# Second GEMM of the last two chunks as Strassen products of 128x256, behind the last first-GEMM sums

## The chip, the cores and the metric

The program runs on one core of a Trainium2 chip. The metric is device time in microseconds of one execution; the kernel before has a median of 893.36 us over three runs (893.23 to 894.0).

## The reference

Windowed attention (8 batches, 8 heads, 576 positions, 64 channels; half of the heads see 32 neighbours, half every fourth of 128) gives 4608 tokens of 512 channels, and these go through a feed-forward block:

```python
x = attn_out.transpose(0, 2, 1, 3).reshape(4608, 512)
h = x @ w_in                                          # w_in 512 x 2048
sp = np.maximum(h, 0.0) + np.log1p(np.exp(-np.abs(h)))
g = h * erf(sp)
out = g @ w_out                                       # w_out 2048 x 512
```

## The kernel before, in words

The tokens are cut into 9 chunks of 512 (`NCH`, `TOK`), the 2048 middle channels into 16 tiles of 128, taken in 8 pairs (`SPC = 8`). Every fp32 operand is held as a high and a low part in float32r, and a product of two operands is three matmuls: high x high, high x low, low x high. Each matmul carries its own load of 128x128 weights.

Chunks 0 to 2 are done plainly, together with most of the attention. Chunks 3 to 8 are done two at a time (`DOUBLES = 3`). For such a pair of chunks and one pair of channel tiles ("a double", `d` = 0 to 23, eight of them for each pair of chunks) the first GEMM `h = x @ w_in` is a Strassen-Winograd product: 7 products instead of 8, each 6 matmuls of 128x512, so 42 matmuls. `mm1_big(d, k)` issues product `k` into one of two PSUM banks, `h` and `bank` (called tx), in turn; `take_big(d, k)` adds it into the results on VectorE. `argument_big` is the softplus on ScalarE, then comes an Erf (both load a table first, since each needs another one), and `multiply_big` makes `g` in place. Of each double the tensor "A" belongs to the first chunk of the two and "B" to the second; B is stored to DRAM (`kept_g`) and read back later (`load_g`).

The second GEMM is plain: an item ("A", d) or ("B", d) is split into `ghi` and `glo` (`split_item`: ScalarE casts B, VectorE subtracts) and takes 24 matmuls of 128x512 into the four banks `acc`, which hold one chunk's 512 tokens by 512 outputs over the 8 items of a chunk.

The order is written out by hand in `period(i, late)`. Period `i` issues item `ITEMS[i]`'s 24 matmuls in four quarters of 6, and where `BIG` names a double for it also that double's 42 matmuls between the quarters. The doubles of the last pair of chunks (d = 16 to 23) are in periods 32 to 39, beside the items ("B", 14), ("B", 15) of the chunk pair before them and the first A items of their own; periods 40 to 49 hold only the ten items that are left. `AFT` names jobs that are put into periods: loads and sums of the right-hand operands of the next eight doubles. All large transfers are issued on SP's queue in program order; `load_left` brings a double's left operands (1.8 MB) two doubles ahead.

The program's functions that the change touches, with what calls them:

Of the kernel before, what the change touches and what calls it, by code (L numbers as in the profile page):

```python
# [139 lines left out]
def attn_moe_kernel(ctx: ExitStack, tc: tile.TileContext, qk, v, masks, eye, w_in, w_out, out):  # L140
# [630 lines left out]
    def take_big(d, k):  # L771
        y = (h, bank)[(7 * d + k) % 2]
# [30 lines left out]
    def multiply_big(kind_, d):  # L803
        e = hs[kind_, d]
        nc.vector.tensor_tensor(out=e, in0=e, in1=ls[kind_, d], op=ALU.mult)
# [319 lines left out]
```

## Time and profile before

| what | value |
|---|---|
| median of three runs | 893.36 us |
| the profiled execution | 892.89 us, of it a span of 890.9 us |
| granted TensorE clock, mean | 0.996 |
| TensorE matmul busy | 871.2 us, 98% |
| weight loads, beside it | 700.1 us, 79% |
| VectorE, ScalarE | 633.6 us (71%), 564.5 us (63%) |

The profile's times are those of one execution and count from its first instruction; the span ends with the last transfer. A matmul's recorded duration (390 ns for 128x512) is longer than its place in the stream, since matmuls are pipelined: what one costs is the distance between two starts. The profile calls the two banks of the first GEMM h and tx, those of the attention sp, and the four of the second GEMM acc.

### The profile page before, as it was taken

How to read it: one execution, taken by the hardware profiler on the slowest of the kernel's cores; microseconds unless marked ns; L12 is line 12 of the kernel's file. 1: busy time of each engine (PE TensorE's matmuls, PEld its weight loads, DVE VectorE, ACT ScalarE, POOL GpSimd, SP SyncE). 2: the span in 40 equal slices, each digit the busy share in tenths (PEclk: the TensorE clock that was granted, in tenths of full speed). 3: DMA queues.
4: the chain of work that ended last, by engine and by line, in shares of the span. 5: the costliest groups of instructions: out<-in, count | busy, mean ns of one | idle time of the engine just before them, and what ended most of it. 6: DMA issues, size and time to landing. Idle time of an engine off the chain costs nothing.

```text
span 890.9 us, 20870 instructions
## 1 busy us (share of the span) xinstructions
PE 871.2 (98%) x8134; PEld 700.1 (79%) x8134; DVE 633.6 (71%) x1575; ACT 564.5 (63%) x1271; POOL 81.3 (9%) x97
## 2 busy tenths in 40 slices
PE   7799999999999999999999999999999999999998
PEld 3367888888888888788887778888888888888886
DVE  5878888987798889777676765666566647576622
ACT  6889888897788886675677442774445434445321
POOL 2312201111111110011000000010000000000000
PEclk9999999999999999999999999999999999999999
DMA  8874446464658896566675741674449125442341
GB/s 272 295 245 154 128 155 197 148 232 127 222 203 270 295 341 248 172 224 221 204 239 200 272 176 54 209 237 161 166 155 361 51 83 200 166 154 83 140 144 48
DMA packets 66915, 170.41 MB, mean 191 GB/s; under 512 B 7680, under 2 KB 14592, under 8 KB 63744
## 3 DMA queue, kind: packets, MB, share of 16 engines
q1 hardware_dynamic: 66528, 168.55, 55.1%
q8 instruction: 64, 1.05, 0.5%
q10 hardware_dynamic: 288, 0.52, 0.2%
q14 instruction: 35, 0.29, 0.1%
HBM read 122.91 MB, written 46.14 MB: 190 GB/s over the span
## 4 chain that ended last, share of the span: by engine, by line
PE 91%; DVE 5%; DMA 1%; ACT 1%; issue 1%; POOL 1%; SPq 0%; DVEq 0%; POOLq 0%; ACTq 0%
PE acc L636 43%; PE h L768 13%; PE tx L768 13%; PE h L521 7%; PE tx L521 7%; PE sp L275 3%; PE sp L217 3%; PE sp L256 1%; PE h L357 1%; DMA qk<-in_qk_dram 1%; DMA v<-in_v_dram 1%; DVE w L458 0%; DVE w L459 0%; DVE prob L228 0%; DVE win L453 0%
## 5 line engine op out<-in xcount | busy, mean ns | idle before, releaser
L636 PE MATMUL acc<-wout_hi,ghi 128*128 128x512 f32 x576 | 227.4, 395 | 0.5 <-DVE ghi L611 0.4
L636 PE MATMUL acc<-wout_lo,ghi 128*128 128x512 f32 x576 | 224.6, 390 | 0.0
L636 PE MATMUL acc<-wout_hi,glo 128*128 128x512 f32 x576 | 159.0, 389 | 0.0
L636 PEld LDWEIGHTS acc<-wout_hi,ghi 128*128 128x128 f32 x576 | 108.2, 188 | 23.3 <-DVE ghi L611 0.9
L636 PEld LDWEIGHTS acc<-wout_hi,glo 128*128 128x128 f32 x576 | 108.1, 188 | 22.8
L636 PEld LDWEIGHTS acc<-wout_lo,ghi 128*128 128x128 f32 x576 | 108.2, 188 | 21.7
L251 POOL TENSOR_TENSOR prob<-prob,rinv 128x256 f32<-128x256 f32 x72 | 72.7, 1016 | 477.0 <-DVE ssum L249 239.9
L238 ACT ACTIVATE prob<-prob,nmax 128x64 f32<-128x64 f32 x288 | 96.3, 338 | 10.5 <-DVE nmax L228 10.3
L801 ACT ACT_TABLE_LOAD x24 | 30.8, 1283 | 93.0 <-DVE dbl L776 47.3
L768 PE MATMUL tx<-win 128*128 128x512 f32 x288 | 74.1, 392 | 0.8 <-DVE hc L778 0.8
L228 DVE CUSTOM_DVE_ANT_0 prob<-sp,cst 128x64 f32<-128x64 f32 x288 | 45.3, 220 | 40.6 <-ACT rows L317 28.2
L768 PE MATMUL h<-win 128*128 128x512 f32 x288 | 74.0, 392 | 0.0
L768 PEld LDWEIGHTS tx<-win 128*128 128x128 f32 x288 | 53.5, 188 | 12.7 <-DVE hc L778 1.2
L768 PEld LDWEIGHTS h<-win 128*128 128x128 f32 x288 | 53.4, 188 | 12.0 <-DVE dbl L778 0.8
L612 DVE TENSOR_TENSOR glo<-hc,ghi 128x512 fp32r<-128x512 f32 x50 | 34.5, 692 | 33.4 <-PE acc L636 22.6
L238 ACT ACTIVATION_READ_ACCUMULATOR prob<-prob,nmax 128x1 f32 x288 | 54.7, 190 | 0.0
L612 DVE TENSOR_TENSOR glo<-dbl,ghi 128x512 fp32r<-128x512 f32 x48 | 33.4, 696 | 28.3 <-PE acc L636 15.6
L521 PE MATMUL h<-x,win 128*128 128x512 f32 x192 | 48.8, 396 | 0.0
L877 ACT ACTIVATE s<-s 128x1024 f32<-128x1024 f32 x48 | 48.2, 1052 | 0.3
L521 PE MATMUL tx<-x,win 128*128 128x512 f32 x192 | 48.0, 392 | 0.0
L801 ACT ACTIVATE s<-hc 128x1024 f32<-128x1024 f32 x24 | 25.5, 1061 | 34.9 <-DVE hc L776 22.8
L611 ACT CAST ghi<-hc 128x512 fp32r<-128x512 f32 x24 | 14.9, 623 | 50.0 <-PE acc L636 41.9
(146 smaller groups left out, 1519.7 us busy)
## 6 DMA issues: line engine op xcount, KB each, us to landing
win<-ws SPq DMA_DIRECT2D x24, 1024.0 KB, 5.0
v<-in_v_dram SPq DMA_DIRECT2D x72, 256.0 KB, 4.9
win<-ws SPq DMA_DIRECT2D x24, 768.0 KB, 5.1
qk<-in_qk_dram SPq DMA_DIRECT2D x48, 272.0 KB, 4.8
dbl<-in_w_in_dram SPq DMA_DIRECT2D x16, 512.0 KB, 4.4
dbl<-in_w_out_dram SPq DMA_DIRECT2D x16, 512.0 KB, 3.9
ws<-x SPq DMA_DIRECT2D x32, 256.0 KB, 4.3
qk<-in_qk_dram SPq DMA_DIRECT2D x24, 288.0 KB, 4.3
```

Of the source, the lines that this page charges most:

```text
L217: nc.tensor.matmul(sps[h][r * STRIP:(r + 1) * STRIP, i, p, :], qkz[i][hs, s * STRIP:(s + 1) * STRIP], qkz[i][hs, at:at + KEYS], start=True ...
L228: nc.vector.tensor_tensor_reduce(out=pr[:, g, :], in0=sps[h][:, u % 2, p, :], in1=mask[QUADS.index(kinds(u, p))], scale=-SCALE, scalar=HUG ...
L238: nc.scalar.activation(out=probs[u][:, j, :], in_=probs[u][:, j, :], func=AF.Exp, scale=-1.0, bias=nmax[:, j:j + 1], accum_out=sums[u][:, ...
L251: nc.gpsimd.tensor_tensor(probs[u], probs[u], rinv.broadcast_to([P, 2 * PARTS, KEYS]), op=ALU.mult)
L275: nc.tensor.matmul(xp[h * D:(h + 1) * D, qs], vt[ks, s, h, :], pt[ks, h * P + s * STRIP:h * P + (s + 1) * STRIP], start=True, stop=True, t ...
L521: nc.tensor.matmul((h, bank)[j], win_at[:, ftp, j, cc // 2, w, cc % 2, :], x[cc], start=(k == 0 and i == 0), stop=(k == CC - 1 and i == 2))
L611: (copy or nc.vector.tensor_copy)(out=ghi, in_=e)
L612: nc.vector.tensor_tensor(out=glo, in0=e, in1=ghi.bitcast(F32), op=ALU.subtract)
L636: nc.tensor.matmul(args["out"], args["lhsT"], args["rhs"], start=args["start"], stop=args["stop"])
L768: nc.tensor.matmul(bank_, w[:, wi, c, :], x[c][:, xi, :], start=(c == 0 and n == 0), stop=(c == 1 and n == 2))
L801: nc.scalar.activation(out=ls[kind_, d], in_=hs[kind_, d], func=AF.Softplus)
L877: nc.scalar.activation(out=e, in_=e, func=AF.Erf)
```

## The change

1. The second GEMM of the last two chunks (16 items of 24 matmuls of 128x512, 384 in all) becomes a Strassen-Winograd product. A step `s` takes one chunk (`kind_`), one half of its tokens (`half`, 256 of them) and one quarter of the middle channels (`q`); it has 7 products, each 6 matmuls of 128x256 (`sums_product`). Over four steps the 7 products gather in 7 of the 8 PSUM banks; in the fourth step they are combined into the outputs (`sums_out`). 16 steps of 42 are 672 matmuls of 128x256. The left operands of a step are sums of quarters of `g` (`row_sums`), split into high and low (`operands`); both are made two steps ahead.
2. The right operands are sums of quarters of `w_out`. They are made for the 8 pairs `p` of channel tiles in `sub_whole`, `sub_sums`, `sub_split`, from period 9 on, stored in DRAM (`wd`), and read back into `win` when that is free (`load_sums`); the pair p = 7 stays on chip until `sub_place`.
3. All of this needs A and B of all eight doubles first, so the doubles 16 to 23 now stand alone (`final(d)`), with no second-GEMM matmuls between their products; the items ("B", 14) and ("B", 15) that stood beside them come behind them (`rest_steps`). A of the last doubles is stored to DRAM as B is.
4. From double 12 on, `h` rotates over four banks (h, tx and the two of the attention), and the first of the 7 products is copied by ScalarE instead of VectorE.
5. In the second half of the run the loads of B11 and B21 for the last doubles are issued three quarters of a period later.

```diff
+FIN = DOUBLES - 1
+FREED = FIN * SPC - 4
+QUART = SPC // 2
+LASTS = [(kind_, half, q) for kind_ in "AB" for half in range(2) for q in range(QUART)]
...
-    kept_g = [dram.tile([SPC, P, PAIR, TOK], F32, name=f"g{i}") for i in range(DOUBLES)]
+    kept_g = {("B", i): dram.tile([SPC, P, PAIR, TOK], F32, name=f"g{i}") for i in range(DOUBLES)}
+    kept_g["A", FIN] = dram.tile([SPC, P, PAIR, TOK], F32, name="ga")
...
-        first, then = (("B11", "B21"), ("B12", "B22")) if k == 1 else (("B12", "B22", "B11", "B21"), ())
+        first, then = (("B11", "B21"), ("B12", "B22")) if k == 1 else (("B12", "B22"), ("B11", "B21"))
...
+    i = 2 * SPC * FIN
+    SUB_AT = {0: ((9, 0), (11, 0), (13, 0), (13, 0)), 4: ((i - 9, 0), (i - 9, 1), (i - 9, 3), (i - 6, 3)),
+              5: ((i - 7, 0), (i - 5, 0), (i - 3, 0), (i - 3, 0)), 6: ((i - 1, 0), (i - 1, 3))}
+    SUB_AT.update({p: ((i - 13 + p, 0), (i - 13 + p, 1), (i - 13 + p, 3), (i - 13 + p, 3)) for p in (1, 2, 3)})
...
-    ITEMS = [NT - 2, NT - 1] + [(kind_, i * SPC + k) for i in range(DOUBLES) for kind_ in "AB" for k in range(SPC)]
+    ITEMS = [NT - 2, NT - 1] + [(kind_, i * SPC + k) for i in range(FIN) for kind_ in "AB" for k in range(SPC)]
+    ITEMS, REST = ITEMS[:-2], ITEMS[-2:]
+
+    def bank_of(d, k):
+        return (h, bank, *spb)[(7 * d + k) % (4 if d >= FREED else 2)]
...
         if k == 0:
-            nc.vector.tensor_copy(out=a[:, 1], in_=y)
+            (nc.scalar.copy if d >= FREED else nc.vector.tensor_copy)(out=a[:, 1], in_=y)
...
+    def sums_product(s, k):
+        q = s % QUART
+        y, (xh, xl) = bank_at(s, k), operand(s, k)
+        for j in range(2):
+            at_, (wh, wl) = slice(j * P, (j + 1) * P), right(2 * q + j)[k]
+            for n, (x, w) in enumerate(((xh, wh), (xh, wl), (xl, wh))):
+                nc.tensor.matmul(y, x[:, at_], w, start=(q == 0 and j == 0 and n == 0),
+                                 stop=(q == QUART - 1 and j == 1 and n == 2))
...
+    def final(d):
+
+        chain = d > FIN * SPC
+        for k in range(4):
+            mm1_big(d, k)
+            take_big(d, k)
+            if k == 0 and chain:
+                for kind_ in "AB":
+                    e = ls[kind_, d - 1]
+                    nc.scalar.activation(out=e, in_=e, func=AF.Erf)
+        load_left(NT + d + 2, 0)
+        if chain:
+            multiply_big("A", d - 1)
+        mm1_big(d, 4)
+        take_big(d, 4)
+        jobs(HALFWAY.get(d - FIN * SPC, ()))
+        argument_big("A", d)
+        if chain:
+            multiply_big("B", d - 1)
+        for k in (5, 6):
+            mm1_big(d, k)
+            take_big(d, k)
+        argument_big("B", d)
+        load_left(NT + d + 2, 1)
+        jobs(LATE.get(d - FIN * SPC, ()))
...
+    LATE = {0: [(sub_split, 6), (sub_store, 6)], 1: [(sub_whole, 7)], 2: [(sub_sums, 7), (load_e, 0, room_halves)],
+            3: [(row_sums, 0, room_w)], 4: [(operands, 0, 0), (operands, 0, 1)],
+            5: [(operands, 0, 2), (operands, 0, 3), (load_rest,)], 6: [(load_sums, 0), (load_sums, 1)],
+            7: [(load_e, 1, lambda: slab(1)), (load_sums, 2), (load_sums, 3)]}
+    HALFWAY = {7: [(split_rest, 0, 0), (split_rest, 0, 1)]}
+
+    def rest_steps():
...
+            if n == 0:
+                for kind_ in "AB":
+                    nc.scalar.activation(out=ls[kind_, d], in_=ls[kind_, d], func=AF.Erf)
+            quarter()
+            quarter()
+            if n == 0:
+                split_rest(1, 0)
+                multiply_big("A", d)
+                multiply_big("B", d)
+                es[3] = [hs["A", i][:, :, 0:HN] for i in (d - 1, d)]
+                load_sums(4)
+            else:
+                row_sums(1, room_s)
+                operands(1, 0)
+            quarter()
+            quarter()
+            if n == 0:
+                split_rest(1, 1)
+            else:
+                operands(1, 1)
+                operands(1, 2)
+        load_e(2, lambda: work.tile([P, PAIR, TOK], F32, name="hc"))
+        store(done(REST[-1]))
+        load_sums(5)
+        load_sums(6)
+
+    def sums_step(s):
+        last_ = s % QUART == QUART - 1
+        for g, ks in enumerate(GROUPS):
+            for k in ks:
+                sums_product(s, k)
+            if s == 0 and g == 0:
+                operands(1, 3)
+            if g == 0:
+                row_sums(s + 2, room_s)
+            if last_:
+                for k in ks:
+                    sums_out(s, k)
+            operands(s + 2, g)
+        load_e(s + 4, lambda: room_e(s + 4))
+        if s == 1:
+            sub_place(SPC - 1)
...
         for i in range(len(ITEMS)):
             period(i, late)
+        for d in range(FIN * SPC, DOUBLES * SPC):
+            final(d)
+        rest_steps()
+        for s in range(len(LASTS)):
+            sums_step(s)
```

Two places show what moves. The first is TensorE in one of the doubles 16 to 23. Before, products of the double (L768) alternate with matmuls of an item (L636):

```order
L768 MATMUL h<-x_99,win 128x512 x3
L768 MATMUL h<-x_100,win 128x512 x3
L768 MATMUL tx<-x_97,win 128x512 x3
L768 MATMUL tx<-x_98,win 128x512 x3
L636 MATMUL acc_93<-wout_hi,ghi 128x512
L636 MATMUL acc_93<-wout_lo,ghi 128x512
L636 MATMUL acc_94<-wout_hi,ghi 128x512
L636 MATMUL acc_94<-wout_lo,ghi 128x512
L636 MATMUL acc_95<-wout_hi,ghi 128x512
L636 MATMUL acc_95<-wout_lo,ghi 128x512
L768 MATMUL h<-dbl_5065,win 128x512 x3
L768 MATMUL h<-plain,win 128x512 x3
```

In the changed kernel the products (now L791) follow each other over four banks; the last of double 23 stand directly ahead of the first of the items that come behind (L642):

```order
L791 MATMUL tx<-x_99,win 128x512 x3
L791 MATMUL tx<-x_100,win 128x512 x3
L791 MATMUL sp_90<-x_97,win 128x512 x3
L791 MATMUL sp_90<-x_98,win 128x512 x3
L791 MATMUL sp_91<-dbl_5067,win 128x512 x3
L791 MATMUL sp_91<-plain,win 128x512 x3
L642 MATMUL acc_93<-wout_hi,ghi 128x512
L642 MATMUL acc_93<-wout_lo,ghi 128x512
```

The item matmuls that stood between a double's products are gone from there, and the double's own products have the time until the bank comes round again. The second place is ScalarE at the end of double 23 and in `rest_steps`: copy of the first product (L801), Erf of double 22 (L1157, with its table), casts of item ("B", 14) (L617), softplus of double 23 (L824, with its table), Erf of double 23 (L1207, with its table), then the casts of item ("B", 15) and those of step 1's operands (L1087):

```order
L801 COPY hc<-tx 128x512
L1157 ACT_TABLE_LOAD
L1157 ACTIVATE s<-s 128x1024 x2
L617 CAST ghi<-w 128x512 x2
L824 ACT_TABLE_LOAD
L824 ACTIVATE s<-hc 128x1024 x2
L1207 ACT_TABLE_LOAD
L1207 ACTIVATE s<-s 128x1024 x2
L617 CAST ghi<-w 128x512 x2
L1087 CAST plain<-dbl_9094 128x512
```

Before, the last softplus and Erf (L801, L877) are followed by casts (L611) and evacuations (L672) of items alone:

```order
L801 ACT_TABLE_LOAD
L801 ACTIVATE s<-hc 128x1024 x2
L877 ACT_TABLE_LOAD
L877 ACTIVATE s<-s 128x1024 x2
L611 CAST ghi<-dbl_9172 128x512
L672 COPY w<-acc_94 128x512
L672 COPY w<-acc_96 128x512
```

So the casts of item ("B", 15), on which TensorE's second plain item rests, now stand behind the Erf of the last double.

More of the change, by code (lines that the diff above doesn't have):

```diff
@@ L771, in take_big @@
     def take_big(d, k):
[L772 removed]
+        y = bank_of(d, k)
         if k == 0:
@@ L922, in attn_moe_kernel, with less, sub_room @@
     pending = []
+    wd = dram.tile([SPC, P, 2, 2, TOK], F32, name="wd")
+    subs, wider = {}, {}
+    def less(out, a, b, op=ALU.subtract):
+        nc.vector.tensor_tensor(out=out, in0=a, in1=b, op=op)
+    def sub_room(p):
+        if p == 0:
+            r, hi = (work.tile([P, PAIR, TOK], F32, name="s") for _ in range(2))
+            return [r[:, j] for j in range(2)], [hi.bitcast(F32R)[:, j] for j in range(2)]
+        if p == SPC - 1:
+            return [work.tile([P, HN], F32, name="prob", bufs=LAG + 1) for _ in range(4)], None
+        r = [work.tile([P, S], F32, name="rows", bufs=4)[:, 0:TOK] for _ in range(2)]
+        return r, [one.tile([P, QW + KW if p % 2 else TOK], F32R, name=f"{('v', 'qk')[p % 2]}{j}")[:, 0:TOK]
+                   for j in range(2)]
@@ new lines, in sub_whole, with sub_sums @@
+    def sub_whole(p):
+        subs[p] = sub_room(p)
+        n = len(subs[p][0]) // 2
+        for i, r in enumerate(subs[p][0]):
+            at_ = (slice(None), 2 * p + i // n, slice(i % n * HN, i % n * HN + r.shape[-1]))
+            less(r, wout_hi[at_].bitcast(F32), wout_lo[at_].bitcast(F32), ALU.add)
+    def sub_sums(p):
+        r, his = subs[p]
+        b11, b12, b21, b22 = r if len(r) == 4 else [t[:, n * HN:(n + 1) * HN] for t in r for n in range(2)]
+        less(b11, b12, b11)
+        less(b12, b22, b12)
+        less(b22, b22, b11)
+        less(b21, b22, b21)
+        for t, hi in zip(r, his or ()):
+            nc.scalar.copy(out=hi, in_=t)
@@ new lines, in attn_moe_kernel, with load_e, room_e @@
+    es, rs, ops = {}, {}, {}
+    GROUPS = ((0, 1), (2, 3), (4, 5), (6,))
+    def load_e(s, room):
+        if s < len(LASTS):
+            kind_, half, q = LASTS[s]
+            es[s] = room()
+            for k in range(2):
+                to = es[s][k] if isinstance(es[s], list) else es[s][:, k].rearrange("p (j n) -> p j n", j=PAIR)
+                nc.sync.dma_start(out=to,
+                                  in_=kept_g[kind_, FIN][2 * q + k][:, :, half * HN:(half + 1) * HN])
+    def room_e(s):
+        return work.tile([P, PAIR, TOK], F32, name="hc") if s % 2 else slab(1 - s // 2 % 2)
@@ new lines, in room_s, with op_room @@
+    def room_s():
+        t = work.tile([P, PAIR, TOK], F32, name="s")
+        return [t[:, 0], t[:, 1]]
+    def op_room(s):
+        if s % 2 == 0:
+            return [work.tile([P, S], F32R, name="rows", bufs=4)[:, 0:TOK] for _ in range(4)] + [
+                one.tile([P, QW + KW], F32R, name=f"qk{i}")[:, 0:TOK] for i in range(2)] + [
+                one.tile([P, TOK], F32R, name="v0")]
+        wide = [io.tile([P, PAIR, TOK], F32R, name=n, bufs=1) for n in ("plain", "dbl2")]
+        return [w[:, j] for w in wide for j in range(PAIR)] + [
+            one.tile([P, TOK], F32R, name="v1"), one.tile([P, TOK], F32R, name="pT1"),
+            work.tile([P, TOK], F32R, name="ghi")]
```

135 lines of the change are left out of this document (130 added, 5 removed).

## The prediction

> **What bounds the kernel now.** I read the page first, then the chain that ended last in order of time, then windows, then single instructions. The page (busy time and share by engine; the chain's shares) names TensorE:
>
> ```profile
> PE 871.2 (98%) x8134; PEld 700.1 (79%) x8134; DVE 633.6 (71%) x1575; ACT 564.5 (63%) x1271; POOL 81.3 (9%) x97
> PE 91%; DVE 5%; DMA 1%; ACT 1%; issue 1%; POOL 1%; SPq 0%; DVEq 0%; POOLq 0%; ACTq 0%
> ```
>
> The chain in order of time (start, length, what) shows the two ends of the stretch that changes:
>
> ```profile
> 667.06 46.24 PE acc L636 x204
> 830.26 57.13 PE acc L636 x252
> ```
>
> Period 32, the first with a double of the last two chunks, begins at 667.06 + 46.24 = 713.30, and the matmul stream ends at 830.26 + 57.13 = 887.39. Between lie 8 x 66 + 10 x 24 = 768 matmuls of 128x512 in 174.1 us, 226.7 ns each; 57.13/252 is 226.7 ns too. So TensorE never waits there, and a saved column is saved time while the others keep up. They have room (stretch, length, busy PE, PEld, DVE, ACT, POOL, clock, DMA share, GB/s):
>
> ```profile
> 501.00:541.00 40.00, 39.52 (x172) 31.80 (x171) 26.96 (x43) 17.12 (x31) 0.00 (x0) 1.00 0.52 182
> 639.60:654.60 15.00, 15.00 (x68) 12.43 (x67) 9.70 (x13) 6.74 (x7) 0.00 (x0) 1.00 0.45 159
> 669.50:713.30 43.80, 43.80 (x195) 36.28 (x194) 28.54 (x45) 21.32 (x34) 0.00 (x0) 1.00 0.55 199
> 713.30:833.00 119.70, 119.70 (x530) 99.12 (x529) 75.73 (x102) 51.80 (x49) 0.00 (x0) 1.00 0.38 132
> 833.00:888.00 55.00, 54.38 (x240) 44.68 (x239) 18.97 (x27) 16.11 (x24) 0.00 (x0) 1.00 0.33 113
> ```
>
> **The price of a 128x256 matmul with its own weights.** 384 matmuls of 512 columns become 672 of 256: seven eighths of the columns, 288 weight loads more. No fp32r matmul of 256 columns is in the trace. The nearest rows (timeline of TensorE and its weight loads, and groups):
>
> ```profile
> 700.22 0.39 PE L636 MATMUL acc<-wout_lo,ghi 128*128 128x512 f32 x1
> 700.22 0.19 PEld L636 LDWEIGHTS acc<-wout_hi,ghi 128*128 128x128 f32 x1
> 700.45 0.39 PE L636 MATMUL acc<-wout_hi,ghi 128*128 128x512 f32 x1
> 385.18 0.60 PE L256 MATMUL sp<-ident,prob 128*128 128x128 f32 x4
> L256 PE MATMUL sp<-ident,prob 128*128 128x128 f32 x114 | 17.4, 273 | 1.0 <-DVE nmax L228 1.0
> 385.51 0.19 PEld L636 LDWEIGHTS acc<-wout_hi,ghi 128*128 128x128 f32 x1
> 385.62 0.19 PEld L636 LDWEIGHTS acc<-wout_lo,ghi 128*128 128x128 f32 x1
> 5.05 1.47 PE L357 MATMUL h<-plain 128*128 128x512 bf16 x6
> L357 PE MATMUL h<-plain 128*128 128x512 bf16 x6 | 1.5, 381 | 0.0
> ```
>
> A weight load starts with the matmul ahead of it and runs beside it (700.22). Its recorded 0.19 us is not its place in the stream: two stand 0.11 us apart behind the transposes (385.51, 385.62), and four transposes, with as many weights but 128 columns, start (0.60 - 0.27)/3 = 0.11 us apart. So weights set a floor of 110 ns. Columns: bf16 matmuls of 512 start (1.47 - 0.381)/5 = 218 ns apart, fp32r ones 226.7. If those 9 ns are paid per matmul and the rest per column, 256 columns take 109 + 9 = 118 ns; if all scales, 113; the ceiling is the full-width 226.7. I take 118, since columns and weights (110) run side by side and the 118 is the larger: 672 x 0.118 = 79.3 us. The ends, 110 and 226.7 ns, give 73.9 and 152.3.
>
> The Trainium skill, "TensorE: Matmul & The Clock Gate", Part 3 (Packing small matmuls), speaks against this change: it says that a weight load overlaps matmuls in flight only where their row groups differ. With the same page's 107 ns for 128 columns of weights, loads would then stand ahead of 107 to 109 ns of columns, and 672 x 0.215 would be 144 us. The rows at 700.22 contradict it for full width. Part 2 of that page gives 262 cycles, 109 ns, for 256 columns back to back, by which the sum would be 73.4; its 216 ns for 512 is below the 226.7 measured here, so I don't take it.
>
> **The doubles 16 to 23 alone:** 8 x 42 x 0.2267 = 76.2 us, if the other engines hold 9.5 us for each. Prices:
>
> ```profile
> 742.51 0.68 DVE L672 COPY o<-acc 128x512 f32<-128x512 f32 x1
> 743.11 0.68 DVE L672 COPY w<-acc 128x512 f32<-128x512 f32 x1
> 740.32 1.22 DVE L805 TENSOR_TENSOR dbl<-dbl,s 128x1024 f32<-128x1024 f32 x1
> 744.72 1.28 ACT L877 ACT_TABLE_LOAD   x1
> 746.02 2.01 ACT L877 ACTIVATE s<-s 128x1024 f32<-128x1024 f32 x2
> 669.33 1.06 ACT L801 ACTIVATE s<-hc 128x1024 f32<-128x1024 f32 x1 [3.39 <-DVE hc L776]
> L611 ACT CAST ghi<-hc 128x512 fp32r<-128x512 f32 x24 | 14.9, 623 | 50.0 <-PE acc L636 41.9 <-DMA hc<-g 6.7 <-issue 1.4
> ```
>
> VectorE: five sums of 512 columns (0.60 apart), one of 1024 and two multiplications (1.2 each), 6.6 us; the jobs put behind the doubles add at most 3.2 (the row sums of step 0 behind double 19: eight operations of 128 columns, each under the 0.40 us that 256 take in a row below), and 1.2 to 1.6 in others. ScalarE: copy 0.6, two tables 2.6, Erf 2.0, softplus 2.1: 7.3, and 1.15 of operand casts in two doubles. Both are under 9.5, but they hang together. By the order of `final`, counted from a double's start: ScalarE copies product 0 when softplus B of the double before is out (2.6 to 3.2), table 4.5, Erf A 5.6 and B 6.5; VectorE ends product 3's sum at 6.3, multiplies A to 7.4, product 4's sum 8.1, multiplies B to 9.2, sums of products 5 and 6 to 10.4 and 11.0; softplus B ends at 12.1, which is 2.6 behind the last product (9.5), so it repeats. Product 5, out at 8.2, is taken 2.2 us late. A bank comes round after four products, and its reader has 4.1 us: TensorE doesn't wait (0), covered by the four banks; with the casts of step 0 ahead the lag grows to 3.3.
>
> Those casts behind doubles 20 and 21 push the end of softplus B from 2.6 to 3.6 us by double 22, and the casts and splits of item ("B", 14) in double 23 (1.05 and 1.2 us) to 4.2.
>
> **The two plain items behind them:** 48 x 0.2267 = 10.9 us, plus a wait. Counted from the last product of double 23: softplus B until 4.2, table and Erf until 7.5, cast of ("B", 15) until 8.1, so TensorE can start that item at 8.2; it finished ("B", 14) at 5.4. That costs 2.75 us. The second half's low part stands behind two multiplications on VectorE (8.7 + 2.4 + 0.6 = 11.7), wanted at 8.2 + 2.7 + 0.45 = 11.4: 0.35 more. Together 3.1 us; the ends are 0 (the chain runs ahead of my count) and 5.
>
> **The 16 steps:** 42 x 0.118 = 5.0 us each. VectorE's prices at 256 columns:
>
> ```profile
> L540 DVE TENSOR_TENSOR plain<-plain 128x256 f32<-128x256 f32 x4 | 1.6, 402 | 0.0
> L541 DVE TENSOR_TENSOR plain<-plain 128x256 f32<-128x256 f32 x4 | 2.6, 647 | 0.1
> ```
>
> Four row sums and a small split 5 x 0.4, three splits 1.8: 3.8 us a step, and 8 x 0.4 for the outputs in every fourth: 18.4 us in four steps against 19.8 of TensorE. It just holds (0 added); ScalarE's four casts are 2.3 us. Operands are made two steps ahead, so a late one has 5 us of grace.
>
> **Transfers.** A double moves 1.8 MB of left operands and now two stores of 0.5 MB: 2.9 MB in 9.5 us, 303 GB/s.
>
> ```profile
> q1 hardware_dynamic: 66528, 168.55, 55.1%
> win<-ws SPq DMA_DIRECT2D x24, 1024.0 KB, 5.0
> ```
>
> 168.55 MB took 55.1% of 890.9 us, so all engines busy would move 343 GB/s. A left half is issued 13.6 us ahead of its use and lands in 5; SP's queue has the stores ahead of it, which wait for multiplications that end before that. I take 0; the end is 3 us.
>
> **Earlier periods.** Seven pairs of w_out's sums cost VectorE 4.0 us each (four operations of 512, four of 256) and ScalarE 1.2, and 1 MB of stores, in periods that have 13 free us of 40 (501 to 541), 5 of 15 (639 to 655) and 15 of 44 (669 to 713) on VectorE. In periods of 5.4 us a job can push a split past its start: between 0 and eight such jobs x 1.2; I take 0.4, since each has a period's lead. The later loads of B11 and B21 still have two periods before their first use: 0. ScalarE's copy in place of VectorE's for d from 12 on: 0, it has 8 us free in 15.
>
> **Tail.**
>
> ```profile
> 886.99 0.39 PE L636 MATMUL acc<-wout_hi,glo 128*128 128x512 f32 x1
> 887.42 0.59 ACT L672 COPY w<-acc 128x512 f32<-128x512 f32 x1 [0.77 <-PE acc L636]
> 888.03 0.34 ACTq L674 DMA_DIRECT2D out_dram<-w  x1
> ```
>
> From 887.42 a 0.59 copy, then the store until 890.9. Now a 0.4 subtraction and half the bytes: 0.2 less.
>
> **Sum:** 76.2 + 10.9 + 3.1 + 79.3 = 169.5 against 174.1: 4.6 less; 0.4 more before, 0.2 less behind: 4.4 less. The profiled execution took 892.89, with 2.0 us around its span of 890.9; the median of the runs is 0.5 higher, 893.4. Forecast: 889.0.
>
> **Rivals.**
> Weights not hidden at half width (slower). Place: every one of the 672 matmuls. For it: a load's 110 ns leave 8 ns of 118, so any delay shows. Against: loads start with the matmul ahead. It decides from 118 + 4.4/0.672 = 124.5 ns on; at 130 the time is 897, in full series (110 + 107) 955.
>
> The rest of a matmul scales with width (113 ns; at the floor 110): 3.4 to 5.4 us less, 883.6 to 885.6. Nothing in the trace excludes it, one width only being there.
>
> VectorE bounds the steps: from 0.45 us an operation of 256 columns on (28 of them and 7.2 us in four steps against 19.8). L541's 0.65 speaks for it, L540's 0.40 against. At 0.5 us: 1.4 us in four steps, 5.6 in all: 894.6.
>
> Something is late that I took as covered: left operands at 303 of 343 GB/s, or splits pushed by the sums of w_out. About 3.5 us: 892.5.
>
> **Chances.** Forecast 0.47, scaling 0.16, weights shown 0.11, VectorE 0.13, lateness 0.13. A difference under 0.2%, 1.8 us, can't be told from none. Faster (under 891.6): 0.43 + 0.16 + 0.02 = 0.61; same 0.20 (0.04 of the forecast, 0.09 of VectorE, 0.07 of lateness); slower 0.19. The range 885 to 895 leaves out the weights and the far ends of scaling and VectorE, 0.2. The likeliest case alone spans 887 to 891.5.
>
> **What would show it.** Starts of the 128x256 matmuls 118 ns apart (a sum of 79 us from the first to the last); no gap between products of doubles 17 to 23; one gap of 2 to 3 us ahead of the second plain item, released by ScalarE's cast; VectorE near 90% in the steps. Wrong, if the products stand 125 ns or more apart, if gaps ended by VectorE lie between the steps, or if TensorE waits for left operands.

## The result, and the profile after

The changed kernel takes 901.69 us (median of four runs, 900.37 to 904.04) beside 893.3 us of the kernel before on the same chip: the ratio is 1.0098, with a 95% interval from 1.0074 to 1.0122. It is slower, where the forecast was 889.0 us and faster. The profiled execution took 902.16 us, with a span of 900.4.

On its page (busy times, the shares of the chain by engine, the granted clock in tenths, and SP's queue with its packets, megabytes and share), these lines answer to those of before:

```profile
PE 871.0 (97%) x8422; PEld 711.4 (79%) x8422; DVE 695.3 (77%) x1747; ACT 604.4 (67%) x1353; POOL 80.0 (9%) x97
PEclk9899999999999999999999999999999999998999
q1 hardware_dynamic: 82464, 191.63, 62.3%
PE 80%; DMA 7%; DVE 7%; ACT 3%; issue 2%; SPq 1%; POOL 0%; DVEq 0%; ACTq 0%; POOLq 0%
```

TensorE's busy time is as before though it streams fewer columns: over the changed stretch it is 173.2 us (the four windows below), where 167.7 would do, so part of the loss is counted as busy. The chain tells more: TensorE's share fell from 91% to 80%, DMA's rose from 1% to 7%, and the clock has a dip near the end that before did not have.

The windows over the changed stretch (stretch, length, busy PE, PEld, DVE, ACT, POOL, clock, DMA share, GB/s) cut it into the doubles 16 to 23, the two plain items, the first three steps with a part of the fourth, and the other steps:

```profile
714.87:793.69 78.82, 77.43 (x338) 62.76 (x337) 58.06 (x85) 55.21 (x60) 0.00 (x0) 1.00 0.80 278
793.69:808.34 14.65, 11.51 (x49) 8.85 (x48) 9.51 (x14) 9.12 (x12) 0.00 (x0) 1.00 0.73 228
808.34:832.39 24.05, 19.57 (x135) 18.86 (x134) 13.27 (x36) 7.79 (x20) 0.00 (x0) 0.86 0.92 327
832.39:897.03 64.64, 64.64 (x541) 64.59 (x539) 52.03 (x119) 26.14 (x51) 0.00 (x0) 1.00 0.32 101
```

From the first matmul of double 16 to the end of the last one's place in the stream are 182.2 us, where the kernel before had 174.1. Without any wait, and at the 120 ns that a 128x256 matmul takes (below), it would be 336 x 0.2267 = 76.16, 48 x 0.2267 = 10.88 and 672 x 0.120 = 80.64: 167.7 us. So 14.5 us are waits and lost clock: 2.65 in the doubles, 3.8 in the plain items and 8.05 in the steps. The steps' loss lies all ahead of 832: the sixteen steps take 5.02, 6.29 and 11.87 us and then 5.04 each. Besides, double 16 begins at 714.87 where the kernel before has 713.14, 1.7 us later (the forecast's 713.30 is where the recorded end of the matmul ahead lies, and its 887.39 the recorded end of the last one). The tail behind the last matmul's place is 3.3 us where it was 3.7.

**Price of the narrow matmul.** The timeline of TensorE has the first two of them:

```profile
808.34 0.28 PE L1110 MATMUL h<-wout_hi,rows 128*128 128x256 f32 x1
808.46 0.28 PE L1110 MATMUL h<-wout_lo,rows 128*128 128x256 f32 x1
```

They start 120 ns apart, as 620 of the 672 do, and the thirteen undisturbed steps of 5.04 us give 5.04/42 = 120 ns too. The weight loads, which stood 110 ns apart in the rows of before, are hidden.

**Doubles.** The waits of ScalarE (715 to 760) and of TensorE (715 to 794; us in total, times, longest) and then one piece of the chain:

```profile
ACT dbl L801 <- DMA ga<-dbl: 2.6, 1, 2.6
PE h L791 <- ACT dbl L801: 0.7, 1, 0.7
```

```profile
731.88 7.33 DMA ga<-dbl
```

The tensor A of double 18 shares its buffer with that of double 16 (both are dbl here). ScalarE's copy of product 0 (L801) writes into it, so it needs the store of the old A (ga<-dbl) to have landed. That store was issued behind 1 MB of left operands in SP's queue and landed 7.33 us later. ScalarE waited, and then TensorE for the bank, first in double 18 and again in later ones; by the starts of its matmuls it lost 2.65 us.

**Plain items.** ScalarE's timeline, and TensorE's wait:

```profile
798.45 1.28 ACT L1207 ACT_TABLE_LOAD   x1
799.74 2.00 ACT L1207 ACTIVATE s<-s 128x1024 f32<-128x1024 f32 x2
801.65 1.12 ACT L617 CAST ghi<-w 128x512 fp32r<-128x512 f32 x2
```

```profile
PE acc L642 <- ACT ghi L617: 3.0, 1, 3.0
```

The cast of item ("B", 15) stands behind the table and the Erf of double 23, and TensorE waits 3.0 us for it.

**Steps.** SP's timeline (DMA issues; the second number is the time of issuing), SP's wait and the pieces of the chain at that place:

```profile
814.10 1.18 SPq L1026 DMA_DIRECT2D hc<-ga  x2
816.02 1.86 SPq L680 DMA_DIRECT2D out_dram<-w  x3
817.97 2.70 SPq L1006 DMA_DIRECT2D win<-wd  x4
```

```profile
SPq L1026 <- DMA g<-hc: 7.0, 1, 7.0
```

```profile
805.28 8.76 DMA g<-hc
818.80 7.84 DMA win<-wd
```

The operand of step 2 is read back into the buffer (hc) of the last B. Its load (L1026, 814.10) cannot be issued until the store of that B (g<-hc, 805.28) has landed, and this took 8.76 us. SP's queue is in order, so all that stands behind waited with it: four stores of outputs, and the sums of w_out for the pairs 5 and 6 (817.97), which need nothing from hc. The second of these four transfers, for which TensorE waited, landed at 826.64. What TensorE waited for (794 to 832; the 3.0 us in the items aside):

```profile
PE sp L1110 <- DMA win<-wd: 2.4, 1, 2.4
PE h L1110 <- ACT rows L1087: 1.1, 1, 1.1
PE h L1110 <- DVE rows L953: 1.0, 1, 1.0
```

Counted from where the next matmul was due, the gaps come to 5.4 us of the 8.05. The rest is in the clock. Windows cut to match its changes, and one from the wait in the plain items:

```profile
800.50:803.90 3.40, 1.59 (x7) 1.33 (x8) 1.61 (x2) 2.67 (x5) 0.00 (x0) 1.00 0.94 251
817.56:820.97 3.41, 1.51 (x11) 1.09 (x9) 1.96 (x5) 1.31 (x3) 0.00 (x0) 1.00 0.99 351
820.97:824.38 3.41, 3.14 (x13) 2.85 (x13) 3.34 (x12) 1.37 (x4) 0.00 (x0) 0.50 0.88 253
824.38:827.80 3.42, 1.11 (x9) 1.11 (x10) 3.42 (x11) 2.76 (x8) 0.00 (x0) 1.00 1.00 369
827.80:831.21 3.41, 3.41 (x18) 3.41 (x18) 1.05 (x4) 0.62 (x1) 0.00 (x0) 0.50 1.03 363
```

After 3.41 us with 1.51 us of work and after 3.42 us with 1.11, the next 3.4 us run at half the clock; after the 3.40 us with 1.59, in the items, they did not. At half clock a matmul takes about 213 ns, 94 more than at full speed; some 28 matmuls were slowed so, 2.6 us. The Trainium skill, "TensorE: Matmul & The Clock Gate", Part 1 (The HAM clock gate), describes a free-running window of 3413 ns and half rate after an idle one. The length agrees with the rows; but in this trace no window was idle, and none of the waits in the two windows was longer than 2.4 us.

### The profile page after: what moved, and what is told of

Read it like the earlier page. It is cut to its first block, busy times and chain, and to the rows that moved or that the text cites. A ratio compares the mean times of both kernels' runs of the same rounds, so it can differ in the third digit from the quotient of the medians.

```text
span 900.4 us, 21932 instructions
## 1 busy us (share of the span) xinstructions
PE 871.0 (97%) x8422; PEld 711.4 (79%) x8422; DVE 695.3 (77%) x1747; ACT 604.4 (67%) x1353; POOL 80.0 (9%) x97
## 3 DMA queue, kind: packets, MB, share of 16 engines
q1 hardware_dynamic: 82464, 191.63, 62.3%
## 4 chain that ended last, share of the span: by engine, by line
PE 80%; DMA 7%; DVE 7%; ACT 3%; issue 2%; SPq 1%; POOL 0%; DVEq 0%; ACTq 0%; POOLq 0%
PE acc L642 29%; PE h L791 8%; PE tx L791 8%; PE h L527 7%; PE tx L527 7%; PE sp L791 4%; PE acc L1110 4%; PE sp L281 3%; PE sp L223 3%; PE sp L1110 2%; DMA ga<-dbl 2%; PE sp L262 1%; DMA g<-hc 1%; DMA dbl<-in_w_in_dram 1%; PE tx L1110 1%
## 5 line engine op out<-in xcount | busy, mean ns | idle before, releaser
L642 PE MATMUL acc<-wout_hi,ghi 128*128 128x512 f32 x448 | 178.3, 398 | 4.4 <-ACT ghi L617 3.0
L642 PE MATMUL acc<-wout_lo,ghi 128*128 128x512 f32 x448 | 174.9, 390 | 0.0
L642 PE MATMUL acc<-wout_hi,glo 128*128 128x512 f32 x448 | 124.0, 390 | 0.1
L642 PEld LDWEIGHTS acc<-wout_hi,ghi 128*128 128x128 f32 x448 | 84.2, 188 | 24.1 <-ACT ghi L617 4.8
L642 PEld LDWEIGHTS acc<-wout_hi,glo 128*128 128x128 f32 x448 | 84.1, 188 | 18.5 <-DVE glo L618 0.5
L642 PEld LDWEIGHTS acc<-wout_lo,ghi 128*128 128x128 f32 x448 | 84.2, 188 | 16.5
L791 PE MATMUL tx<-win 128*128 128x512 f32 x216 | 55.8, 394 | 0.8 <-DVE hc L801 0.8
L791 PE MATMUL h<-win 128*128 128x512 f32 x216 | 55.8, 393 | 0.0
L791 PEld LDWEIGHTS tx<-win 128*128 128x128 f32 x216 | 40.0, 188 | 9.9 <-DVE hc L801 1.2
L791 PEld LDWEIGHTS h<-win 128*128 128x128 f32 x216 | 39.9, 188 | 9.2 <-DVE dbl L801 0.7
L323 ACT COPY rows<-sp 128x128 f32<-128x128 f32 (+7 forms) x167 | 27.5, 308 | 27.9 <-PE sp L223 27.4
L824 ACT ACTIVATE s<-dbl 128x1024 f32<-128x1024 f32 x24 | 25.5, 1061 | 27.5 <-DVE dbl L799 27.4
L527 PEld LDWEIGHTS h<-x,win 128*128 128x128 f32 x192 | 35.4, 188 | 8.0
L527 PEld LDWEIGHTS tx<-x,win 128*128 128x128 f32 x192 | 35.7, 188 | 7.5
L824 ACT ACTIVATE s<-hc 128x1024 f32<-128x1024 f32 x24 | 25.5, 1061 | 20.4 <-DVE hc L799 18.1
```

What stands on the lines that cost most here:

```text
L323: nc.scalar.copy(out=to, in_=src)
L527: nc.tensor.matmul((h, bank)[j], win_at[:, ftp, j, cc // 2, w, cc % 2, :], x[cc], start=(k == 0 and i == 0), stop=(k == CC - 1 and i == 2))
L642: nc.tensor.matmul(args["out"], args["lhsT"], args["rhs"], start=args["start"], stop=args["stop"])
L791: nc.tensor.matmul(bank_, w[:, wi, c, :], x[c][:, xi, :], start=(c == 0 and n == 0), stop=(c == 1 and n == 2))
L824: nc.scalar.activation(out=ls[kind_, d], in_=hs[kind_, d], func=AF.Softplus)
```

## The experiments

Two theories stood at first. One: the loss is order, that is, transfers stand in SP's queue behind a transfer or a wait which they don't need, and another order takes the loss away. The other: it is rate, the 16 DMA engines being full, so that a repair at one place only moves the wait to the next. All edits are against the changed kernel unless another is named. The table is in us; the last three columns are what each profiled execution took over 76.16, 10.88 and 80.64. The executions reach the end of the attention up to 3 us apart (607.65 to 610.67), so the start of double 16 alone doesn't tell what the periods ahead of it cost; the column beside it does, from the last matmul of the attention (sp<-pT,v) to the first of double 16. The kernel before takes 103.64 us there.

| kernel | median | before beside it | ratio, 95% interval | start of double 16 | attention to double 16 | doubles | items | steps |
|---|---|---|---|---|---|---|---|---|
| changed | 901.69 | 893.3 | 1.0098, 1.0074 to 1.0122 | 714.87 | 105.94 | 2.65 | 3.8 | 8.05 |
| e1_step2_early | 895.67 | 893.04 | 1.0035, 1.0018 to 1.0053 | 714.77 | 105.98 | 2.43 | 4.75 | 0.4 |
| e2_no_left_loads | 897.94 | 893.04 | 1.0070, 1.0045 to 1.0095 | 715.60 | 106.11 | 0 | 4.4 | 5.4 |
| e3_casts_ahead_of_erf | 899.49 | 893.04 | 1.0086, 1.0066 to 1.0106 | 714.80 | 105.69 | 1.5 | 2.2 | 7.7 |
| e4_stores_first | 900.92 | 893.04 | 1.0098, 1.0077 to 1.0120 | 716.18 | 106.01 | 0 | 6.1 | 6.4 |
| e5_three_repairs | 896.0 | 892.55 | 1.0040, 1.0027 to 1.0054 | 715.19 | 105.86 | 0 | 0.1 | 7.6 |
| e6_early_sums_moved | 895.33 | 892.55 | 1.0027, 1.0012 to 1.0043 | 713.15 | 105.32 | 0 | 0 | 7.7 |
| e7_two_banks | 906.45 | 892.55 | 1.0148, 1.0106 to 1.0190 | 718.54 | 107.87 | 10.6 | 0 | 6.3 |
| e8_loads_without_waits | 890.97 | 893.37 | 0.9975, 0.9962 to 0.9988 | 712.97 | 105.32 | 0 | 0 | 3.4 |
| e9_all_repairs | 886.78 | 892.26 | 0.9937, 0.9923 to 0.9950 | 712.72 | 103.64 | 0 | 0 | 1.1 |

**The load of step 2 ahead, into a free buffer** (e1_step2_early):

```diff
-            7: [(load_e, 1, lambda: slab(1)), (load_sums, 2), (load_sums, 3)]}
+            7: [(load_e, 2, lambda: [x.bitcast(F32)[:, :, 0:HN] for x in xs[2:4]]),
+                (load_e, 1, lambda: slab(1)), (load_sums, 2), (load_sums, 3)]}
...
-        load_e(2, lambda: work.tile([P, PAIR, TOK], F32, name="hc"))
```

> The half-tensors of step 2 are loaded into the free tiles x2 and x3 right behind double 23, not into an hc tile that has to wait until the store of B of double 23 has landed; nothing else is changed. Theory Q (the order of SP's queue: that one wait held back this load and the last sums of w_out behind it, and TensorE's wait then halved its clock): the 24.05 us of steps 0 to 2 up to 832.4 fall by some 7 to 8, all 128x256 matmuls stand 120 ns apart, clock 1.00 in the steps; about 894 us. Rival W (the DMAs are simply full at 92% there and move what they can): the same bytes land at about the same time, 5 us or more of the loss stay; 898 to 901.

The windows of the items and of the steps:

```profile
793.36:808.99 15.63, 12.57 (x49) 10.00 (x48) 10.48 (x16) 9.52 (x12) 0.00 (x0) 0.89 0.85 277
808.99:890.03 81.04, 80.94 (x673) 80.68 (x671) 64.51 (x158) 32.84 (x70) 0.00 (x0) 1.00 0.47 165
```

The steps now take 81.04 us: of 8.05 us lost, 0.4 are left, and the clock stays at 1.00 there. The same bytes go; only one load stands elsewhere and waits for nothing. The items got 1 us worse, by a half clock of 3.4 us in them (0.89). So in the changed kernel the steps' loss hung on the wait in SP's queue. The time, 895.67, is 1.7 us above the 894 expected.

**No left operands for the last doubles** (e2_no_left_loads). It leaves out the loads of the left operands of the doubles 18 to 23, which then compute with old data:

```diff
-        load_left(NT + d + 2, 0)
...
-        load_left(NT + d + 2, 1)
```

> Leaves out the loads of the left operands of doubles 18 to 23, so these doubles compute with old operands (11 MB of transfers less in the 79 us of doubles 16 to 23). If late stores hold TensorE in those doubles (theory T: ScalarE's copy of product 0 waits for the store of A two doubles back, which lands 6 to 7 us after its issue instead of 3), their 2.7 us of waits go to 0.3 or less, and with shorter landings behind them the wait in step 2 shrinks to under 2 us: 891 to 893. Rival C (ScalarE's and VectorE's own chain from double to double is too long): 2 us or more of the waits in the doubles stay, and only the later part gets shorter: 894 or more.

```profile
715.60:791.76 76.16, 76.16 (x338) 63.09 (x336) 58.47 (x86) 55.51 (x60) 0.00 (x0) 1.00 0.40 148
```

With the DMA share down from 0.80 to 0.40, TensorE doesn't wait once in the doubles. So it was the transfers, and neither VectorE nor ScalarE by themselves. The steps still lose 5.4 us, where under 2 were expected, and the time is 897.9 and not 891 to 893: their loss is not a leftover of the doubles' traffic.

**Stores ahead of the next left operands** (e4_stores_first) moves no byte out, only the order:

```diff
-        load_left(NT + d + 2, 0)
         if chain:
             multiply_big("A", d - 1)
...
             multiply_big("B", d - 1)
+        load_left(NT + d + 2, 0)
```

> In doubles 16 to 23 the first 1 MB of left operands is issued behind the two stores of the double before, not ahead of them. Theory T with the queue's order (a store lands late because 1 MB stands ahead of it): the stores of A land in 4 us instead of 6 to 7 and the 2.7 us of waits in the doubles go to under 0.7: 899. Rival (the rate: DMA share 0.80 over the doubles, order doesn't matter): landings stay at 6 us and the waits at 2 us or more; 901 to 902.

The windows of the doubles and items, and, from the DMA issues of both kernels (715 to 793), the stores of A with their median us to landing:

```profile
716.18:792.34 76.16, 76.16 (x338) 63.09 (x336) 58.10 (x85) 55.24 (x60) 0.00 (x0) 1.00 0.81 289
792.34:809.29 16.95, 14.07 (x50) 11.02 (x49) 11.23 (x17) 9.39 (x12) 0.00 (x0) 0.80 0.72 235
```

```profile
ga<-dbl SPq DMA_DIRECT2D x4, 512.0 KB, 6.1
```

```profile
ga<-dbl SPq DMA_DIRECT2D x4, 512.0 KB, 3.4
```

At the same share of DMA (0.81) the doubles lose nothing: the store lands in 3.4 us where it took 6.1 (the first of the two lines is the changed kernel's), and the left half, which had 13.6 us, can bear the delay. In the doubles the cause was order alone. The time fell by only 0.8 us, where 2.7 were expected: the 2.88 us wait in the items, 0.1 us shorter than in the changed kernel, here lay so that the clock halved for 6.8 us from 800.2 on, which cost 2.3 us, and double 16 began 1.3 us later.

**The casts ahead of the Erf** (e3_casts_ahead_of_erf):

```diff
-            if n == 0:
-                for kind_ in "AB":
-                    nc.scalar.activation(out=ls[kind_, d], in_=ls[kind_, d], func=AF.Erf)
             quarter()
             quarter()
             if n == 0:
                 split_rest(1, 0)
+                for kind_ in "AB":
+                    nc.scalar.activation(out=ls[kind_, d], in_=ls[kind_, d], func=AF.Erf)
```

> The cast and split of the second plain item's first half stand ahead of the Erf of double 23 on ScalarE. If ScalarE's order holds TensorE there, as forecast, the 3.6 us lost over the two plain items fall to under 0.8. What comes then is open: if step 2 waits for transfers that land at a set time (theory Q), TensorE just comes to that wait 3 us earlier and waits longer, and the time stays within 1 us of 901.7; if the loss in step 2 hangs on engines (rival), it is 898.5.

The items' loss fell from 3.8 to 2.2 us, not under 0.8, since the second half's cast (`split_rest(1, 1)`) still stood behind the Erf. That the doubles lost 1.5 us here and 2.65 in the changed kernel, with the same code there, is a difference between executions. The time, 899.5, lies between the two that were expected. SP issued the store of the last B at 802.55 instead of 805.28, and step 2's wait ended 3 us earlier with it: its transfers don't land at a set time. The steps still lose 7.7 us.

**All three repairs** (e5_three_repairs): e1, e4, and both splits of the last item ahead of the Erf. The multiplications behind the Erf, and the load of the sums for pair 4, move with it:

```diff
-            if n == 0:
-                for kind_ in "AB":
-                    nc.scalar.activation(out=ls[kind_, d], in_=ls[kind_, d], func=AF.Erf)
...
-                multiply_big("A", d)
-                multiply_big("B", d)
-                es[3] = [hs["A", i][:, :, 0:HN] for i in (d - 1, d)]
-                load_sums(4)
...
             if n == 0:
                 split_rest(1, 1)
+                for kind_ in "AB":
+                    nc.scalar.activation(out=ls[kind_, d], in_=ls[kind_, d], func=AF.Erf)
+                multiply_big("A", d)
+                multiply_big("B", d)
+                es[3] = [hs["A", i][:, :, 0:HN] for i in (d - 1, d)]
+                load_sums(4)
```

> Step 2's half-tensors into x2 and x3, the stores of each double ahead of the left loads, and the casts of the second plain item all ahead of the Erf of double 23. If the three waits are separate causes (theory), they add: doubles 76.2 us (0 to 0.3 of waits), plain items 10.9 plus under 1, steps 80.6 plus under 0.7, clock 1.00 from double 16 on; with a start of double 16 near 714.9 and the same tail the time is 888 to 890, below before. Rival (one wait only hides the next, since the DMAs are near full): what one repair frees comes back in the next place, 3 us or more of waits remain, 892 or more.

The window of the steps, and TensorE's wait:

```profile
802.33:890.58 88.25, 83.31 (x673) 82.86 (x671) 67.69 (x164) 35.27 (x74) 0.00 (x0) 0.96 0.49 171
```

```profile
PE sp L1110 <- DMA win<-wd: 4.4, 1, 4.4
```

Doubles and items are whole, and the steps lose 7.6 us again, now waiting for the sums of w_out. TensorE arrives at the steps 6.7 us earlier than in e1 (802.33 beside 808.99), and the transfer for which it waits only 1.5 us earlier (819.54 beside 821.08): most of what the two repairs gave came back as a wait, as the rival had it. So e1's near zero was partly the shelter of the waits ahead of it.

**The early sums moved** (e6_early_sums_moved, against e5) takes the casts of w_out's sums as a job of their own (`sub_hi`) and spreads the jobs over more periods:

```diff
-    SUB_AT = {0: ((9, 0), (11, 0), (13, 0), (13, 0)), 4: ((i - 9, 0), (i - 9, 1), (i - 9, 3), (i - 6, 3)),
-              5: ((i - 7, 0), (i - 5, 0), (i - 3, 0), (i - 3, 0)), 6: ((i - 1, 0), (i - 1, 3))}
...
+              4: ((i - 9, 0), (i - 8, 3), (i - 7, 0), (i - 6, 0), (i - 6, 3)),
+              5: ((i - 7, 2), (i - 5, 0), (i - 4, 0), (i - 3, 0), (i - 3, 0)), 6: ((i - 1, 0), (i - 1, 3), (i - 1, 3))}
```

> As the one with three repairs, and in periods 23 to 29 the sums of w_out for p = 4 and 5 stand further apart, with ScalarE's casts a period behind VectorE's sums. If these sums hold up the splits of periods 24 to 28 (theory: 1.6 us of gaps in TensorE there, two behind VectorE's late ghi, two behind ScalarE's cast that waits for the sums of p = 5), double 16 starts 1 to 1.7 us earlier and the time is 1 to 1.7 us lower, 886.5 to 889. Rival (the attention before, or transfers, set that start): no change.

The time is 0.7 us below e5's, where 1 to 1.7 were expected. Double 16 begins at 713.15, 2.0 us ahead of e5, but 1.5 us of that this execution was ahead by the end of the attention (607.83 beside 609.33). From there on the move gave back 0.5 us (105.32 beside 105.86), and 1.7 us over the 103.64 of before stay. The steps lose 7.7 us as in e5. One of SP's waits (785 to 800) and two windows show why:

```profile
SPq L1030 <- DMA g<-dbl: 2.6, 1, 2.6
```

```profile
795.00:800.00 5.00, 5.00 (x24) 4.14 (x23) 3.14 (x4) 3.15 (x4) 0.00 (x0) 1.00 0.63 184
805.00:810.00 5.00, 5.00 (x44) 4.99 (x43) 4.89 (x19) 2.16 (x6) 0.00 (x0) 1.00 1.02 415
```

At 805 to 810 the DMA engines are full, at over 400 GB/s. From 795 to 800, ahead of that, they were busy 0.63, and only 0.34 in the first 2 us: until 794.9 SP had waited 2.6 us for the store of the B before the last to land, all later loads stood behind that wait, and the DMA engines ran short of work. The queue had idle room ahead of the place where it was full.

**Loads where they need not wait** (e8_loads_without_waits, against e6): everything that the steps 1 to 3 read is issued right behind double 23, into buffers that are free by then:

```diff
-            7: [(load_e, 2, lambda: [x.bitcast(F32)[:, :, 0:HN] for x in xs[2:4]]),
-                (load_e, 1, lambda: slab(1)), (load_sums, 2), (load_sums, 3)]}
+            7: [(load_e, 1, lambda: [x.bitcast(F32)[:, :, 0:HN] for x in xs[0:2]]), (load_sums, 2), (load_sums, 3),
+                (load_e, 2, lambda: [x.bitcast(F32)[:, :, 0:HN] for x in xs[2:4]]),
+                (load_sums, 4), (load_sums, 5), (load_sums, 6)]}
...
-                load_sums(4)
...
-        load_sums(5)
-        load_sums(6)
```

> As the one with the early sums moved, and all that steps 1 to 3 need (half-tensors of step 1 into x0 and x1, of step 2 into x2 and x3, sums of w_out for p = 2 to 6) is issued right behind double 23, with no store and no evacuation ahead of it that SP would wait for. There the transfers of the kernel before this one run at 200 GB/s and a share of 0.6 (795 to 800 us) and at 410 GB/s and 1.0 from 805 on, while step 2 waits 4.9 us for p = 5. Theory O (order: SP's queue leaves the DMAs part idle while it waits, and then they are full): the waits of step 2 go, steps 80.6 plus under 0.6, 7 us less, 887 to 889 and below before. Rival R (rate alone: so many bytes between double 22 and step 3 can't move in time): 7 MB at 410 GB/s still end after TensorE needs them, 3 us or more of waits remain, 891 or more.

The window of 795 to 800, that of the steps, and VectorE's timeline where they wait:

```profile
795.00:800.00 5.00, 5.00 (x23) 4.13 (x22) 3.54 (x7) 3.44 (x5) 0.00 (x0) 1.00 0.90 309
800.01:884.04 84.03, 81.83 (x673) 80.82 (x671) 67.50 (x169) 34.52 (x74) 0.00 (x0) 1.00 0.49 171
```

```profile
818.81 0.43 DVE L955 TENSOR_TENSOR s<-dbl 128x256 f32<-128x256 f32 x1 [4.55 <-DMA dbl<-ga]
```

The share at 795 to 800 rose from 0.63 to 0.90, and the steps' loss fell from 7.7 to 3.4 us. The kernel is 0.25% faster than before (0.12 to 0.38%), so the gain exists, but at 890.97 us it fell short of the 887 to 889 expected. Step 4 holds 2.5 of the 3.4 us: the same kind of wait one place further on, as its operand is loaded behind stores of outputs and lands at 818.7, and VectorE waits 4.55 us for it. The other 0.9 is in step 0, where TensorE waits for a bank with outputs of the plain items.

**That load ahead as well** (e9_all_repairs, against e8). It also takes the outputs of the plain items out of their banks ahead of step 1's operands, and puts the sums of the pairs 4 and 5 some periods later:

```diff
-              4: ((i - 9, 0), (i - 8, 3), (i - 7, 0), (i - 6, 0), (i - 6, 3)),
-              5: ((i - 7, 2), (i - 5, 0), (i - 4, 0), (i - 3, 0), (i - 3, 0)), 6: ((i - 1, 0), (i - 1, 3), (i - 1, 3))}
+              4: ((i - 9, 0), (i - 6, 0), (i - 5, 0), (i - 4, 0), (i - 4, 3)),
+              5: ((i - 6, 2), (i - 5, 0), (i - 4, 0), (i - 3, 0), (i - 3, 0)), 6: ((i - 1, 0), (i - 1, 3), (i - 1, 3))}
...
+            if n == 1:
+                load_e(4, lambda: slab(1))
+                store(done(item))
...
-        store(done(REST[-1]))
...
-        load_e(s + 4, lambda: room_e(s + 4))
+        if s:
+            load_e(s + 4, lambda: room_e(s + 4))
```

> As the one whose loads have no waits ahead of them, with the three places mended where its trace still shows TensorE waiting: the sums of w_out for p = 4 stand in periods 26 to 28 and not around period 25 (1.4 us of gaps at 675 to 680 us), step 4's half-tensor is asked for ahead of the outputs of the plain items (2.1 us at 822), and these outputs leave the banks ahead of step 1's operands (0.7 us at 803). If these are the last waits, TensorE runs from double 16 to the end in 167.7 us and the time is 885 to 887, 0.7% below before. Rival (VectorE or the full DMAs make new waits of the same size): 889 to 891.

```profile
712.72:788.88 76.16, 76.16 (x337) 63.06 (x336) 58.45 (x86) 55.50 (x60) 0.00 (x0) 1.00 0.81 291
788.88:799.76 10.88, 10.88 (x49) 9.01 (x48) 7.38 (x11) 7.95 (x11) 0.00 (x0) 1.00 0.85 287
799.76:881.52 81.76, 81.36 (x673) 80.74 (x671) 67.42 (x169) 34.15 (x73) 0.00 (x0) 1.00 0.50 176
```

The three stretches take 168.8 us where before has 174.1, and 167.7 is the sum without waits. Step 0 went from 5.93 to 5.03 us and step 4 from 7.55 to 6.17. The way from the attention to double 16 is 103.64 us, as before the change, where e8 has 105.32: 1.7 us of e9's gain lie there, and 2.3 in the steps. At 886.78 us (six runs, 886.19 to 886.97) it is 0.63% faster than the kernel before, with an interval of 0.50 to 0.77%, and beats both kernels. It moves the same 191.63 MB on SP's queue as the changed kernel.

**Two banks in place of four** (e7_two_banks, against e5): h rotates over two banks from double 12 on, and VectorE copies product 0.

```diff
-FREED = FIN * SPC - 4
+FREED = DOUBLES * SPC
```

> As the one with three repairs, but h stays on two banks and VectorE copies product 0 for all doubles. The forecast put TensorE's wait at 0 because of four banks, product 5 being taken 2.2 us late. With two banks its reader has 1.4 us (one product) instead of 4.1, so each of the doubles 17 to 23 should lose 0.8 to 2 us, 6 to 14 us in all: 895 to 903. Rival (the banks don't matter at this pace, VectorE's sums keep up as they did before): doubles at 76.2, 889.

The window of the doubles, and one of the waits there:

```profile
718.54:805.26 86.72, 80.25 (x338) 61.62 (x337) 64.11 (x94) 51.97 (x53) 0.00 (x0) 1.00 0.73 261
```

```profile
PEld tx L791 <- DVE dbl L811: 3.5, 4, 1.0
```

The doubles lose 10.6 us where e5 loses none, ended by VectorE: most by its sums (L811), some by its copy of product 0 (L801). So the four banks, with ScalarE's copy, are what covers the doubles that stand alone. Which of the two does it was not run apart. Double 16 begins 3.4 us later too, 2.0 of them lost behind the attention (107.87 beside 105.86). The time, 906.45, is past the 903 expected, which counted from 889, where e5 took 896.0.

## Why the prediction was wrong, point by point

- **Width.** 118 ns taken, 120 measured: 672 x 2 ns = 1.3 us more. The mechanism was right: a share per column and a share per matmul (226.7 - 120 = 106.7 ns for 256 columns more, which leaves 13.3 ns per matmul) and hidden weights. Two widths alone would fit any such split, but the stretches at half clock bear it out: there 256 columns stand 213 ns apart (828 to 831) and 512 columns 427 (e4, 801 to 806), twice 106.7 and twice 213.3 (226.7 - 13.3), with nothing per matmul. The rivals of weights that show (124.5 ns and more) and of plain scaling (113) are both excluded. The rule of the Trainium skill, "TensorE: Matmul & The Clock Gate", Part 3, that loads overlap only across row groups, doesn't hold here at half width either; the 109 ns of its Part 2 are too low.
- **VectorE in the steps.** No wait taken, and from the fourth step on there is none, at 52.03 of 64.64 us busy (80%, not near 90%). This rival fell.
- **Transfers: "I take 0".** This is the step that failed; the end named there was 3 us, and 2.65 in the doubles and 8.05 in the steps came. It failed three times over. It compared 303 GB/s with 343, a capacity worked out from a mean over the span; in the steps over 400 GB/s moved (415 in e6), so rate was not where that figure put it. It asked if loads arrive in time, and not what their place in the queue does to stores: a store landed in 7 to 9 us, not in the 3.4 of e4, and two readers needed that landing, ScalarE's copy of product 0 and step 2's load. And the steps' own loads were costed at nothing without a look at what stands ahead of them on SP; the lateness rival had the mechanism in words, with 3.5 us as its price, a third of these 10.7 us.
- **Doubles: TensorE doesn't wait.** Right for the engines (no wait in e2 and e4), and the four banks with ScalarE's copy cover it (e7). The wait that came was a transfer's.
- **The plain items.** 3.1 us taken, 3.8 measured, with the releaser that was forecast. By the starts of the matmuls 3.3 of it are the wait for the cast, where 2.75 were taken, and 0.4 the one for the second half's low part, where 0.35 were. e5 takes it to 0.1.
- **Earlier periods: 0.4, "since each has a period's lead".** 2.3 us measured; double 16 is only 1.7 later because this execution was 0.6 ahead at the end of the attention. The windows from there to double 16, of the kernel before, the changed one, e6 and e9, and two waits of the changed kernel (640 to 715):

```profile
609.50:713.14 103.64, 103.64 (x472) 85.80 (x465) 66.56 (x95) 48.31 (x64) 0.00 (x0) 1.00 0.51 179
608.93:714.87 105.94, 104.97 (x472) 85.42 (x465) 85.51 (x136) 56.31 (x78) 0.00 (x0) 1.00 0.64 215
607.83:713.15 105.32, 104.54 (x473) 85.57 (x466) 85.62 (x136) 56.11 (x78) 0.00 (x0) 1.00 0.65 216
609.08:712.72 103.64, 103.64 (x472) 85.80 (x465) 85.34 (x136) 55.81 (x78) 0.00 (x0) 1.00 0.66 219
```

```profile
ACT qk L982 <- DVE rows L953: 4.6, 4, 2.4
PE acc L642 <- DVE ghi L617: 0.7, 1, 0.7
```

  TensorE waits twice for an item's cast on VectorE, the first time (671.98) directly behind the sums there (L953), and twice for one on ScalarE, the first time (692.59) directly behind the job's casts (L982), which wait for such sums in the same queue. A mean of free time on VectorE doesn't say that. The move in e6 gave 0.5 us back; the one in e9, with the sums for pair 4 later still, gave back all of it, with VectorE as busy as in the changed kernel.
- **The clock.** It wasn't in the sum. Short waits close together cost 2.6 us more in the steps, and in e1 and e4 1 and 2.3 us in the items (against the changed kernel's).
- **Tail.** 0.2 less taken, 0.4 measured.

Span against forecast, 900.4 - 886.5 (889.0 less 2.0 around the span and 0.5 to the median): 13.9 us, of which 1.3 are width, 2.65 the doubles, 0.7 the items, 8.05 the steps and 1.3 the later start of double 16, less 0.2 in the tail. The gain that the width gives was real: e9 has it, with 5.3 us less from double 16 to the last matmul than before.

It stays open what part of the last 1.1 us in e9's steps is rate (from 797 to 820 the DMA engines are full there, at 392 GB/s), and what a store's landing depends on; both were seen only in this order of transfers.

## What to carry to other kernels

When a change moves transfers, write down for each queue what is issued ahead of a load and which of that must wait, and give a store's landing, not its issue, as the time at which its buffer is free. A mean rate hides both the idle stretch behind a wait in the queue and the full one after it: read the DMA share in windows of 5 us. Repair in order of time and run the repairs together, since a wait that goes shows the next, and a repair that looks complete may stand in the shelter of a wait ahead of it.

## What the runs showed of the hardware

The work within some 3.4 us, and not one long wait, went with TensorE's clock: 1.51 and 1.11 us of work were followed by half the clock for 3.4 us. Cut into such windows at the places where the clock changes, the ten traces of the changed kernel and of e1 to e9 have eleven at full clock with 1.51 us of TensorE's work or less (from 46 us on), and half the clock follows each; only once does it follow more work, 1.87 us (e7, from 64.7 on). The phase matters: the 3.0 us wait in the changed kernel's items left 1.59 us of work and cost no clock, and a wait of 2.88 us in e4 cost 6.8 us at half. Its windows there:

```profile
796.80:800.20 3.40, 1.14 (x6) 0.60 (x4) 0.00 (x0) 3.37 (x5) 0.00 (x0) 1.00 0.20 70
800.20:803.60 3.40, 2.79 (x7) 2.21 (x8) 2.81 (x3) 1.58 (x4) 0.00 (x0) 0.50 0.90 230
803.60:807.00 3.40, 3.40 (x10) 2.63 (x9) 3.37 (x9) 1.26 (x3) 0.00 (x0) 0.50 1.00 281
```

It lay almost whole in one window (1.14 us of work), and the next, itself not full, was followed by a second one at half. The other surprise is the DMA rate: 415 GB/s at a share of 1.02 (e6, 805 to 810), where 343 had been worked out from the page of before.
